# Second softmax group through GpSimd, logit sums on GpSimd, and router choices two per period, in a fused attention and mixture-of-experts kernel

## The chip, the core and the metric

The kernel runs on one core of a Trainium2 chip. The metric is the device time of one execution in microseconds (us), the median of several. The engines named below are TensorE (PE, with its weight loads shown apart as PEld), VectorE (DVE), ScalarE (ACT), GpSimd (POOL) and SyncE (SP, which here only issues DMAs).

## What is computed

Banded causal attention over 8 batches, 8 heads, 576 positions and head width 64 (window 64), and then a mixture of 8 experts over the 4608 tokens of 512 values. Tokens are given to experts by descending logit, each expert taking at most 576.

```python
scores = scale * np.matmul(q, k.transpose(0, 1, 3, 2))
mask = (rel >= 0) & (rel < window)
scores = np.where(mask, scores, -1000000000.0)
scores = scores - np.max(scores, axis=-1, keepdims=True)
attn = np.exp(scores)
attn = attn / (np.sum(attn, axis=-1, keepdims=True) + 1e-09)
x = np.matmul(attn, v)                  # then laid out as (4608, 512)
...
logits = x @ w_gate                     # (4608, 8)
order = np.argsort(-logits.flatten())   # greedy assignment, 576 tokens per expert
...
h = np.maximum(x[mask] @ w1[e], 0.0)    # for each expert e, on its tokens
out[mask] = h @ w2[e]
```

## The kernel before

**Stages.** Attention comes first (the change touches only this stage), then the routing of the first expert, then the products of the experts, with the routing of the later experts beside them. Nothing of the routing of expert 0 can begin before the last logits are there.

**Periods.** Queries are handled in 36 periods m = 0 to 35, two blocks of 64 queries each (one block per half of the 128 partitions), all 8 heads in two groups g = 0 and 1 of four heads. `S` is 576, so a batch b has nine blocks and its first one falls in period 9b/2 (rounded down). The loop is written out by hand as a software pipeline: the order in which it issues instructions is the order in which each engine runs them. In period m it issues:

- `qk(m, g)` (L118): 32 score matmuls on PE (L129); then on DVE, for each of 8 heads, one fused operation (L137) that adds the mask, scales by -1/8, writes `st` and accumulates the minimum into `mx` (so st is the negated scaled score and mx the negated row maximum). `st` has two buffers. A period's DVE work begins with these eight operations; the moment when the eighth has written its `mx` is called T(m) below.
- in some periods the gate products: `gate_mm` (PE, L86) with its copy `gate_cp` (ACT, L90) in the period where a batch begins, and in the next period `gate_tr` (PE, L96) and `gate_out`. The latter copies the products into `VO` (DVE, L102, L105) and then lets GpSimd build `VE`, the same rows of v shifted by one block, in eight copies per batch (`even`, L115 and L116). The periods with `gate_out` of a whole batch, called turning periods below, are 10, 14, 19, 23, 28 and 32 (batches 2 to 7).
- `pv(m - 2)` (PE, L169): 32 products of the exponentials with v. Besides the 64 values, the matmul yields the partial logits of 8 experts (columns 64 to 71) and the sum of the exponentials (column 72), into `Op`, which has one buffer.
- exponentials of group 0 (ACT, L142, one per head, with mx as the bias), `tr(m - 1)` (PE, L149: 8 transposes into `Tp`), and then on ACT two exponentials of group 1, the copy of the first `Tp` to `pt` (L151), two more exponentials, the copy of the second.
- `norm(m - 2)` (DVE): 1/sum (`r`, L198 and L199), the partial logits times r (`l`, L184), in every fourth period the sum over the eight heads into `L` (L188), and the values times r (`x`, L194). Between these four steps the loop puts one small operation each: those of `choices` (six operations on four columns of logits, which prepare the routing: m, G, oh, w, best, one) if any are waiting in `late`, else one of the generator `setup` (constants for the routing: tab, gt, sx, s and the like). At least two of the setup operations go into each period until they run out.
- DMA issues on SP: a store of x to DRAM, and in six periods the loads of a batch that comes later.

Of the kernel before, what the change touches and what calls it, by code (L numbers as in the profile page):

```python
# [9 lines left out]
FT = mybir.dt.float32  # L10
# [4 lines left out]
AF = mybir.ActivationFunctionType  # L15
OP = mybir.AluOpType
AX = mybir.AxisListType
# [5 lines left out]
E = 8  # L23
# [7 lines left out]
def attention(ctx, tc, c, q, k, v, vt, gate, xs, L, choices, setup, counters):  # L31

    nc = tc.nc
    wgbd, wg = gate
    ld = ctx.enter_context(tc.tile_pool(name="ld", bufs=2))
    wk = ctx.enter_context(tc.tile_pool(name="wk", bufs=3))
# [44 lines left out]
    def gate_mm(b, i0, i1):  # L81
        if not i0:
            VS[b] = wk.tile([128, S], FT, name="vs", bufs=2)
        pv = VS[b, i0] = ps.tile([128, 512], FT, name="Tp", bufs=2)
        for p in range(HP):
            nc.tensor.matmul(pv[32 * p:32 * p + 32, :64 * (i1 - i0)], wgbd[:, p, :],  # L86
                             VT[b][:, i0:i1, p], start=True, stop=True)

    def gate_cp(b, i0, i1):
        nc.scalar.activation(VS[b][:, 64 * i0:64 * i1], VS[b, i0][:, :64 * (i1 - i0)], AF.Copy)  # L90

    def gate_tr(b, i0, i1):
        pt = VS[b, i0] = ps.tile([128, 512], FT, name="Tp", bufs=2)
        for n, j in enumerate(range(i0 // 2, (i1 + 1) // 2)):
            w = 128 if j < 4 else 64
            nc.tensor.transpose(pt[:w, 128 * n:128 * n + 128], VS[b][:, 128 * j:128 * j + w], c["ident"])  # L96

    def gate_out(b, i0, i1):
        pt = VS[b, i0]
        j0, j1 = i0 // 2, i1 // 2  # L100
        n = j1 - j0
        nc.vector.tensor_copy(VO[b][:, j0:j1, :, 64:72],  # L102
                              pt[:, :128 * n].rearrange("p (j h g) -> p j h g", j=n, h=8)[:, :, :, :8])
        if i1 % 2:
            nc.vector.tensor_copy(VO[b][0:64, 4, :, 64:72],  # L105
                                  pt[:64, 128 * n:128 * n + 128].rearrange("p (h g) -> p h g", h=8)[:, :, :8])
        if not i0:
            VE[b] = ld.tile([128, 4, H, VW], FT, name="VE")
        for j in range(4):
            if i0 <= 2 * j + 2 < i1:  # L110
                even(b, j, nc.gpsimd if b or j > 1 else nc.vector)
# [6 lines left out]
    def qk(m, g):  # L118

        Sp = [t[g] for t in SP]  # L120
        bi = [divmod(2 * m + a, NB) for a in range(2)]
        for pp in range(2):
            p = 2 * g + pp
            for a, (b, i) in enumerate(bi):

                k0 = i - 1 if i else 0
                for r in range(2):
                    d = slice(64 * r, 64 * r + 64)
                    nc.tensor.matmul(Sp[r][64 * a:64 * a + 64, pp], Q[b][d, i, p],  # L129
                                     K[b][d, k0:k0 + 2, p], start=True, stop=True)  # L130
        kinds = [int(i > 0) for b, i in bi]
        mk = c["mask"][tuple(kinds)]
        st = wk.tile([128, 4, 128], FT, name="st", bufs=2)
        mx = wk.tile([128, 4], FT, name="mx")
        for h in range(4):

            nc.vector.tensor_tensor_reduce(st[:, h, :], Sp[h % 2][:, h // 2], mk, scale=-0.125, scalar=3.0e38,  # L137
                                           op0=OP.add, op1=OP.min, accum_out=mx[:, h:h + 1])
        pe = wk.tile([128, 4, 128], FT, name="pe", bufs=4)

        def exp(h):
            nc.scalar.activation(pe[:, h, :], st[:, h, :], AF.Exp, bias=mx[:, h:h + 1], scale=-1.0)  # L142

        return pe, [lambda h=h: exp(h) for h in range(4)]

    def tr(pe):
        Tp = ps.tile([128, 512], FT, name="Tp", bufs=2)
        for h in range(4):
            nc.tensor.transpose(Tp[:, 128 * h:128 * h + 128], pe[:, h, :], c["ident"])  # L149
        pt = wk.tile([128, 4, 128], FT, name="pt")  # L150
        return pt, lambda: nc.scalar.activation(pt.rearrange("p h q -> p (h q)"), Tp, AF.Copy)  # L151

    stores = []
    late = []
# [20 lines left out]
    def norm(m, Op):  # L175

        r = wk.tile([128, 2, 4], FT, name="r")
        x = wk.tile([128, H, D], FT, name="x", bufs=HOLD + 4)
        if m % 4 == 0:
            XL[0] = wk.tile([128, 4, H, E], FT, name="l", bufs=2)  # L180
        l = XL[0]

        def gates():
            nc.vector.tensor_tensor(l[:, m % 4].rearrange("p (g h) e -> p g h e", g=2), Op[:, :, :, 64:72],  # L184
                                    r[:, :, :, None].to_broadcast([128, 2, 4, E]), OP.mult)
            if m in ends:
                j0 = ends[m]
                nc.vector.tensor_reduce(L[:, j0:m + 1, :], l[:, j0 % 4:m % 4 + 1].rearrange("p i h e -> p i e h"),  # L188
                                        axis=AX.X, op=OP.add)
                if m != 34:  # L190
                    late.extend(choices(min(j0, 32), m + 1))

        def values():
            nc.vector.tensor_tensor(x.rearrange("p (g h) d -> p g h d", g=2), Op[:, :, :, 0:64],  # L194
                                    r[:, :, :, None].to_broadcast([128, 2, 4, 64]), OP.mult)
            stores.append((m, x))

        return [lambda: nc.vector.tensor_scalar(r, Op[:, :, :, 72], 1e-9, None, op0=OP.add),  # L198
                lambda: nc.vector.reciprocal(r, r), gates, values]  # L199
# [17 lines left out]
    def load_all(b):  # L217
        load_qk(b, *ALL)
        load_vt(b, *ALL)
        load_v(b, *ALL)  # L220

    M = B * NB // 2
# [15 lines left out]
    for m in range(M + 1):  # L238
        exps = [[], []]
        if m < M:  # L240
            P[m], exps = zip(*[qk(m, g) for g in range(2)])

        for x in products.get(m, []):
            gate_mm(*x)
        for x in turns.get(m, []):
            gate_tr(*x)
        for x in turns.get(m, []):
            gate_out(*x)
        Op = pv(m - 2, T.pop(m - 2)) if m > 1 else None
        for f in exps[0]:  # L250
            f()
        for x in products.get(m, []):
            gate_cp(*x)
        if m:
            T[m - 1], cps = zip(*[tr(pe) for pe in P.pop(m - 1)])
            for n, f in enumerate(exps[1]):
                f()
                if n % 2:
                    cps[n // 2]()
            if m == M:  # L260
                for f in cps:
                    f()
            if m == 1:
                for x in first:
                    gate_tr(*x)
                for x in first:
                    gate_out(*x)
        else:
            for f in exps[1]:
                f()  # L270
        more = [lambda: next(setup, None)] * (6 if m < 5 else 2)
        ops = norm(m - 2, Op) if Op is not None else []
        for f in ops:
            f()
            if late:
                late.pop(0)()
            elif more:
                more.pop()()
        for f in more:
            f()  # L280
        for s in (2 * m, 2 * m + 1):
            if stores and (len(stores) > HOLD or s > LOADED):
                store(*stores.pop(0))
        for b in loads.get(m, []):
            load_all(b)
# [80 lines left out]
class Routing:  # L366
# [90 lines left out]
    def choices(self, j0, j1, p):  # L457

        nc, V = self.nc, self.V
        r = slice(j0, j1)  # L460
        n = j1 - j0

        def wide(x):
            return x[:, r, None].to_broadcast([128, n, E])

        f = [lambda: nc.vector.tensor_reduce(self.m[:, r], V[:, r], axis=AX.X, op=OP.max),
             lambda: nc.vector.tensor_tensor(self.oh[:, r], V[:, r], wide(self.m), OP.is_equal),
             lambda: nc.vector.scalar_tensor_tensor(self.w[:, r], self.oh[:, r], 9.0,
                                                    self.cw9[:, None, :].to_broadcast([128, n, E]),
                                                    op0=OP.mult, op1=OP.add),  # L470
             lambda: nc.vector.tensor_reduce(self.best[:, r], self.w[:, r], axis=AX.X, op=OP.max),
             lambda: nc.vector.tensor_tensor(self.best[:, r], self.best[:, r], self.un[:, r], OP.mult),
             lambda: nc.vector.tensor_tensor(self.one[:, r], self.w[:, r], wide(self.best), OP.is_equal)]
        if not p:
            f.pop(4)
            f.insert(1, lambda: self.compare(self.G0, self.tab[:, 0], j0, j1))
        return f
# [603 lines left out]
```

## Time and profile before

| | us |
|---|---|
| median of 3 runs (661.39 to 663.77) | 663.59 |
| the profiled execution's own time | 665.81 |
| span of the profiled execution, first to last instruction | 664.2 |
| PE busy (matmul rows) | 623.3 |
| DVE busy | 441.6 |
| ACT busy | 356.9 |
| POOL busy | 187.2 |

The profile cannot chain the waits of this execution back beyond its last 11 us, so the attention stage has to be read from windows and from timelines: the order of instructions of one engine in a stretch, with the idle time before each. The stage runs from the first score matmuls at 4.7 us to the last division at about 161 us; the routing of expert 0 follows, in which PE is mostly idle, and from about 185 us to the end PE is busy without pause.

### The profile page before, as it was taken

To read this page: it belongs to the slowest core of one execution; us is meant where nothing else is said; L and a number is where in the kernel's file an instruction comes from. 1 tells how busy PE (TensorE), PEld (TensorE's weight loads), DVE (VectorE), ACT (ScalarE), POOL (GpSimd) and SP (SyncE) were. 2 spreads that over 40 slices of the span, in tenths; PEclk is the share of its full clock that TensorE was granted. 3 is DMA by queue.
4 is the path that set the end of the run, shared out by engine and by line. 5 is a ranking of instruction groups with operands and counts; after the bars stand their busy time and mean duration, and the time that the engine had idled before them with its cause. 6 is when DMAs were issued, how large, how long until landed. Compare 5 with 4: busy or idle time off the path is not lost. (4 is left out here: it accounts for less than half of the span.)

```text
span 664.2 us, 16832 instructions
## 1 busy us (share of the span) xinstructions
PE 623.3 (94%) x6383; PEld 535.6 (81%) x6383; DVE 441.6 (66%) x2102; ACT 356.9 (54%) x733; POOL 187.2 (28%) x218
## 2 busy tenths in 40 slices
PE   6989999996489999999999999999999999999995
PEld 4767787775379878987997898799889878989984
DVE  7798998887787767876885887588578741311300
ACT  5778898893056166336626543661744356635310
POOL 2223333330062042206305222530612155212111
PEclk9899999998589999999999999999999999999999
DMA  8999999721078189739748875965977598973401
GB/s 315 383 392 380 361 354 360 262 81 66 16 250 194 29 282 225 144 132 253 187 81 292 201 157 182 231 160 107 286 193 144 203 215 254 235 222 87 88 25 47
DMA packets 36016, 134.09 MB, mean 202 GB/s; under 512 B 4696, under 2 KB 4824, under 8 KB 32864
## 3 DMA queue, kind: packets, MB, share of 16 engines
q0 software_dynamic: 15280, 52.98, 35.5%
q1 hardware_dynamic: 20368, 79.52, 32.3%
q8 instruction: 50, 0.82, 0.5%
q10 hardware_dynamic: 288, 0.52, 0.3%
q14 instruction: 30, 0.25, 0.1%
HBM read 82.15 MB, written 18.87 MB: 152 GB/s over the span
## 5 line engine op out<-in xcount | busy, mean ns | idle before, releaser
L961 POOL DMA_INDIRECT out<-ot,idx x40 | 41.7, 1043 | 270.8 <-DVE ot L959 82.2
L911 ACT ACTIVATE hh<-h 128x256 fp32r<-128x256 f32 (+1 forms) x128 | 51.9, 408 | 101.1 <-PE h L939 99.8
L916 DVE SCALAR_TENSOR_TENSOR hl<-h,hh 128x256 fp32r<-128x256 f32 x128 | 53.2, 416 | 76.3 <-ACT hh L911 70.0
L981 PE MATMUL o<-wh,hh 128*128 128x512 f32 x256 | 102.5, 400 | 0.0
L981 PE MATMUL o<-wl,hh 128*128 128x512 f32 x256 | 101.8, 398 | 0.0
L981 PE MATMUL o<-wh,hl 128*128 128x512 f32 x256 | 101.4, 396 | 0.0
L142 ACT ACTIVATE pe<-st,mx 128x128 f32<-128x128 f32 x288 | 92.5, 393 | 14.8 <-DVE mx L137 14.8
L939 PE MATMUL h<-xh,wh 128*128 128x256 f32 (+1 forms) x512 | 92.0, 299 | 2.0 <-issue 1.0
L939 PE MATMUL h<-xh,wl 128*128 128x256 f32 (+1 forms) x512 | 93.0, 299 | 0.0
L939 PE MATMUL h<-xl,wh 128*128 128x256 f32 (+1 forms) x512 | 92.1, 298 | 0.4 <-DVE xl L874 0.4
L939 PEld LDWEIGHTS h<-xh,wh 128*128 128x128 f32 x512 | 75.8, 189 | 3.3 <-issue 1.1
L939 PEld LDWEIGHTS h<-xh,wl 128*128 128x128 f32 x512 | 76.1, 190 | 0.2
L939 PEld LDWEIGHTS h<-xl,wh 128*128 128x128 f32 x512 | 75.7, 190 | 0.7 <-DVE xl L874 0.6
L828 ACT ACTIVATE wh<-st 128x1024 fp32r<-128x1024 f32 x64 | 67.2, 1050 | 5.8 <-DMA st<-w 5.8
L137 DVE CUSTOM_DVE_ANT_0 st<-Sp,mask 128x128 f32<-128x128 f32 x288 | 63.7, 287 | 7.7 <-PE Sp L129 6.7
L839 POOL DMA_DIRECT2D wl<-st x61 | 56.6, 1231 | 35.3 <-ACT wl L837 24.1
L837 ACT ACTIVATE wl<-wh 128x1024 fp32r<-128x1024 f32 x61 | 64.4, 1056 | 0.8
L953 ACT ACTIVATE ot<-o 128x512 f32<-128x512 f32 x32 | 19.1, 598 | 84.1 <-PE o L981 80.9
L981 PEld LDWEIGHTS o<-wh,hl 128*128 128x128 f32 x256 | 48.1, 188 | 9.3 <-issue 0.4
L981 PEld LDWEIGHTS o<-wh,hh 128*128 128x128 f32 x256 | 48.3, 188 | 8.8
L981 PEld LDWEIGHTS o<-wl,hh 128*128 128x128 f32 x256 | 48.2, 188 | 8.6
L880 POOL DMA_INDIRECT xg<-xs,idx x40 | 41.4, 1036 | 45.5 <-DVE eq L724 35.1
(177 smaller groups left out, 1084.7 us busy)
## 6 DMA issues: line engine op xcount, KB each, us to landing
wl<-st POOLq DMA_DIRECT2D x61, 512.0 KB
st<-w SPq DMA_DIRECT2D x60, 512.0 KB
xs<-x SPq DMA_DIRECT2D x36, 256.0 KB
VO<-v SPq DMA_DIRECT2D x6, 1168.0 KB
Q<-q SPq DMA_DIRECT2D x6, 1152.0 KB
K<-k SPq DMA_DIRECT2D x6, 1152.0 KB
VT<-vt SPq DMA_DIRECT2D x6, 1152.0 KB
VO<-v SPq DMA_DIRECT2D x4, 584.0 KB
```

The lines of the kernel that those rows point to most:

```text
L137: nc.vector.tensor_tensor_reduce(st[:, h, :], Sp[h % 2][:, h // 2], mk, scale=-0.125, scalar=3.0e38, op0=OP.add, op1=OP.min, accum_out=mx[ ...
L142: nc.scalar.activation(pe[:, h, :], st[:, h, :], AF.Exp, bias=mx[:, h:h + 1], scale=-1.0)
L828: nc.scalar.activation(hi, st[i], AF.Copy)
L837: nc.scalar.activation(lo, hi.bitcast(FT), AF.Copy, scale=-1.0)
L839: nc.gpsimd.dma_start(lo.bitcast(FT), st[i], accum_op=OP.add)
L880: nc.gpsimd.indirect_dma_start(out=g[0:n, a], out_offset=None, in_=self.xs, in_offset=IndirectOffsetOnAxis(ap=idx[0:n, a:a + 1], axis=0))
L911: nc.scalar.activation(hh[:, f, c0:c1], h, AF.Relu)
L916: nc.vector.scalar_tensor_tensor(t, h[:, a - c0:b - c0], 0.0, hh[:, f, a:b].bitcast(FT), op0=OP.max, op1=OP.subtract)
L939: nc.tensor.matmul(h, wv[:, cc, 128 * (f % 2):128 * (f % 2) + 128], xt[:, cc, c0:c1], start=(k == 0), stop=(k == 11))
L953: nc.scalar.activation(ot, o, AF.Copy)
L961: nc.gpsimd.indirect_dma_start(out=self.out, out_offset=IndirectOffsetOnAxis(ap=idx[0:m, a:a + 1], axis=0), in_=ot[0:m], in_offset=None)
L981: nc.tensor.matmul(o, ht[:, f, 128 * a:128 * a + 128], wt[:, 512 * (f % 2):512 * (f % 2) + 512], start=(k == 0), stop=(k == 23))
```

## The change

Three edits, all within the loop of the attention stage.

**Exponentials of group 1.** In periods 0 to 34 `qk` issues, right behind the DVE operations of group 1, a GpSimd subtraction of mx from st over 128 x 512 elements, into `pe`. ACT then takes the exponential of all 512 columns in one instruction, in place. The loop issues it behind both copies of `Tp` rather than around the first.

**Sum over the heads.** For the 32 first periods three GpSimd additions (256 numbers of a row folded to 128, 64 and 32) take the place of the DVE reduction.

**Choices.** `norm`'s first two steps are followed by setup operations only; a waiting choice operation is put behind `l` and another behind `x`, two per period, and not in the period that produced them.

```diff
-        return pe, [lambda h=h: exp(h) for h in range(4)]
+        if not g or m == M - 1:
+            return pe, [lambda h=h: exp(h) for h in range(4)]
+        nc.gpsimd.tensor_tensor(pe, st, mx[:, :, None].to_broadcast([128, 4, 128]), OP.subtract)
+        return pe, [lambda: nc.scalar.activation(pe.rearrange("p h k -> p (h k)"), pe.rearrange("p h k -> p (h k)"),
+                                                 AF.Exp, scale=-1.0)]
...
-                nc.vector.tensor_reduce(L[:, j0:m + 1, :], l[:, j0 % 4:m % 4 + 1].rearrange("p i h e -> p i e h"),
-                                        axis=AX.X, op=OP.add)
+                if m < 32:
+                    a = wk.tile([128, 4, 4, E], FT, name="a", bufs=1)
+                    nc.gpsimd.tensor_tensor(a, l[:, :, 0:4], l[:, :, 4:8], OP.add)
+                    nc.gpsimd.tensor_tensor(a[:, :, 0:2], a[:, :, 0:2], a[:, :, 2:4], OP.add)
+                    nc.gpsimd.tensor_tensor(L[:, j0:m + 1, :], a[:, :, 0], a[:, :, 1], OP.add)
+                else:
+                    nc.vector.tensor_reduce(L[:, j0:m + 1, :], l[:, j0 % 4:m % 4 + 1].rearrange("p i h e -> p i e h"),
+                                            axis=AX.X, op=OP.add)
...
-            for n, f in enumerate(exps[1]):
+            for f in (*cps, *exps[1]):
                 f()
-                if n % 2:
-                    cps[n // 2]()
-            if m == M:
-                for f in cps:
-                    f()
...
-        for f in ops:
+        ready = len(late)
+        for n, f in enumerate(ops):
             f()
-            if late:
+            if n > 1 and ready:
                 late.pop(0)()
+                ready -= 1
             elif more:
                 more.pop()()
```

What stands in a row on the engines (line numbers of the changed kernel are its own: L147 is the new exponential, L146 the subtraction, L194 to L196 the additions, L155 the copy of `Tp`, L208, L209, L188 and L204 the steps of `norm`, L473 to L488 the choices, L451 to L456 setup). ACT, two periods before, the first of them one in which a batch begins:

```order
L142 ACTIVATE pe<-st,mx 128x128 x4
L90 ACTIVATE vs<-Tp 128x256
L90 ACTIVATE vs<-Tp 128x320
L142 ACTIVATE pe<-st,mx 128x128 x2
L151 ACTIVATE pt<-Tp 128x512
L142 ACTIVATE pe<-st,mx 128x128 x2
L151 ACTIVATE pt<-Tp 128x512
L142 ACTIVATE pe<-st,mx 128x128 x6
```

ACT now, the same place:

```order
L142 ACTIVATE pe<-st,mx 128x128 x4
L90 ACTIVATE vs<-Tp 128x256
L90 ACTIVATE vs<-Tp 128x320
L155 ACTIVATE pt<-Tp 128x512 x2
L147 ACTIVATE pe<-pe 128x512
L142 ACTIVATE pe<-st,mx 128x128 x4
```

The copies of `Tp` stand in front of group 1's exponential, and four instructions have become one. GpSimd now, periods 15 to 20 (batch 4's turning period 19 is among them; three further pairs of copies are left out):

```order
L146 TENSOR_TENSOR pe<-st,mx 128x512 x3
L194 TENSOR_TENSOR a<-l 128x128
L195 TENSOR_TENSOR a<-a 128x4x16
L196 TENSOR_TENSOR L<-a 128x32
L146 TENSOR_TENSOR pe<-st,mx 128x512 x2
L115 COPY VE<-VO 64x584
L116 COPY VE<-VO 64x584
...
L146 TENSOR_TENSOR pe<-st,mx 128x512 x2
```

Before, this engine had only the copies of VE in this stage. The subtraction of period 20 now stands behind the eight copies of period 19. DVE before, behind the eight operations of a turning period (10):

```order
L102 COPY VO<-Tp 128x16x8 x2
L105 COPY VO<-Tp 64x8x8
L198 TENSOR_SCALAR r<-Op 128x8
L467 TENSOR_TENSOR oh<-L,m 128x32
L199 RECIPROCAL r<-r 128x8
L468 SCALAR_TENSOR_TENSOR w<-oh,cw_219 128x32
L184 TENSOR_TENSOR l<-Op,r 128x64
L471 TENSOR_REDUCE best<-w 128x4
L194 TENSOR_TENSOR x<-Op,r 128x512
L473 TENSOR_TENSOR one<-w,best 128x32
L449 TENSOR_TENSOR s_674<-sx_939,sx_1030 72x5
L444 TENSOR_SCALAR sx_1139<-jp 72x4
```

DVE now, the same place:

```order
L102 COPY VO<-Tp 128x16x8 x2
L105 COPY VO<-Tp 64x8x8
L208 TENSOR_SCALAR r<-Op 128x8
L456 TENSOR_TENSOR s_662<-sx_922,sx_1013 72x5
L209 RECIPROCAL r<-r 128x8
L451 TENSOR_SCALAR sx_1115<-jp 72x4
L188 TENSOR_TENSOR l<-Op,r 128x64
L473 TENSOR_REDUCE m<-L 128x4
L204 TENSOR_TENSOR x<-Op,r 128x512
L488 TENSOR_TENSOR G_76<-m,tab 128x60
```

The two setup operations have moved from the end to the places ahead of `l`, and choices come two at a time. In the built program the first DVE operation of a period, which writes group 0's `st`, now waits for GpSimd's subtraction of the period before: the two buffers of `st` are handed on in the order in which they are released, and the subtraction is issued before the exponentials of group 0. Before, both groups' operations waited for ACT.

## Rows read from the trace of the kernel before

**Rows 1.** The profile's page: busy time of the engines, and the span in 40 slices (busy share in tenths; PEclk is TensorE's granted clock).

```profile
PE 623.3 (94%) x6383; PEld 535.6 (81%) x6383; DVE 441.6 (66%) x2102; ACT 356.9 (54%) x733; POOL 187.2 (28%) x218
...
PE   6989999996489999999999999999999999999995
DVE  7798998887787767876885887588578741311300
ACT  5778898893056166336626543661744356635310
PEclk9899999998589999999999999999999999999999
```

**Rows 2.** Busy time of each engine in windows (us, then PE, PEld, DVE, ACT, POOL busy, granted clock, DMA share, GB/s): one plain period, nine periods in a row, the two halves of the loop, the routing of expert 0.

```profile
78.40:81.70 3.30, 3.30 (x77) 2.82 (x74) 2.83 (x23) 3.30 (x11) 0.00 (x0) 1.00 0.91 332
...
75.12:108.51 33.39, 32.88 (x674) 26.38 (x672) 30.26 (x217) 31.46 (x95) 9.65 (x15) 1.00 0.95 346
...
30.97:96.76 65.79, 61.18 (x1236) 48.85 (x1230) 58.91 (x393) 56.58 (x168) 21.69 (x32) 1.00 0.99 372
96.76:151.30 54.54, 52.06 (x1077) 42.09 (x1075) 47.06 (x320) 49.20 (x147) 16.08 (x24) 1.00 0.63 235
...
158.60:185.00 26.40, 11.89 (x329) 10.15 (x326) 19.18 (x97) 1.53 (x2) 1.07 (x1) 0.54 0.17 57
```

**Rows 3.** Timeline of PE's weight loads, periods 20 to 24 (start, duration, line, names; in brackets idle time before and its releaser; rows of `pv` are left out). L149 is `tr`, L86 `gate_mm`, L96 `gate_tr`.

```profile
91.16 0.86 PEld L149 LDWEIGHTS Tp<-ident,pe 128*128 128x128 f32 x8
...
94.39 0.86 PEld L149 LDWEIGHTS Tp<-ident,pe 128*128 128x128 f32 x8
95.42 0.86 PEld L129 LDWEIGHTS Sp<-K,Q 64*64 64x64 f32 x32 [0.17 <-issue]
97.63 0.86 PEld L149 LDWEIGHTS Tp<-ident,pe 128*128 128x128 f32 x8
...
99.69 0.16 PEld L86 LDWEIGHTS Tp<-VT,wgs 128*32 128x32 f32 x8 [0.17 <-ACT pe L142]
...
100.89 0.13 PEld L169 LDWEIGHTS Op<-VE,pt 128*64 128x64 f32 x1 [0.52 <-issue]
...
102.07 0.86 PEld L149 LDWEIGHTS Tp<-ident,pe 128*128 128x128 f32 x8
...
106.19 0.86 PEld L149 LDWEIGHTS Tp<-ident,pe 128*128 128x128 f32 x8
```

**Rows 4.** Timeline of ACT: the start of period 5, a whole plain period (17, with what comes ahead of it), and the start of period 35. Instructions of one kind in a row are merged (x6).

```profile
30.97 1.28 ACT L142 ACTIVATE pe<-st,mx 128x128 f32<-128x128 f32 x4
...
78.43 1.85 ACT L142 ACTIVATE pe<-st,mx 128x128 f32<-128x128 f32 x6
80.18 0.58 ACT L151 ACTIVATE pt<-Tp 128x512 f32<-128x512 f32 x1
80.66 0.69 ACT L142 ACTIVATE pe<-st,mx 128x128 f32<-128x128 f32 x2
81.24 0.59 ACT L151 ACTIVATE pt<-Tp 128x512 f32<-128x512 f32 x1
81.72 1.86 ACT L142 ACTIVATE pe<-st,mx 128x128 f32<-128x128 f32 x6
...
151.30 1.85 ACT L142 ACTIVATE pe<-st,mx 128x128 f32<-128x128 f32 x6
```

**Rows 5.** Waits from 41 to 156 us, sums over the stretch: who waited for whom, us in total, times, longest.

```profile
PEld Op L169 <- issue: 4.6, 13, 1.0
PEld Sp L129 <- issue: 4.1, 16, 1.6
...
PEld Tp L86 <- ACT pt L151: 2.0, 6, 0.4
...
PEld Op L169 <- POOL VE L116: 1.4, 2, 0.7
...
PEld Tp L96 <- ACT pt L151: 1.3, 6, 0.2
```

**Rows 6.** Timeline of GpSimd and DVE around copies of VE: the first copy behind its DVE copy in period 5, then GpSimd's first and last copy of turning period 19.

```profile
32.11 0.28 DVE L102 COPY VO<-Tp 128x128 f32<-128x128 f32 x1
...
32.45 0.67 POOL L115 COPY VE<-VO 64x584 f32<-64x584 f32 x1 [5.91 <-DVE VO L102]
...
90.99 0.67 POOL L115 COPY VE<-VO 64x584 f32<-64x584 f32 x1 [13.41 <-issue]
...
96.05 0.67 POOL L116 COPY VE<-VO 64x584 f32<-64x584 f32 x1
```

**Rows 7.** Timeline of DVE, periods 19 to 21: the end of period 19's eight operations, period 20's `r` and `x`, the first of period 21's eight and the end of the last.

```profile
90.58 0.08 DVE L137 DVE_READ_ACCUMULATOR2_ANT mx<- 128x1 f32 x1
...
94.70 0.16 DVE L198 TENSOR_SCALAR r<-Op 128x8 f32<-128x8 f32 x1
...
95.34 0.67 DVE L194 TENSOR_TENSOR x<-Op,r 128x512 f32<-128x512 f32 x1
96.25 0.29 DVE L137 CUSTOM_DVE_ANT_0 st<-Sp,mask 128x128 f32<-128x128 f32 x1 [0.23 <-PE Sp L129]
...
97.94 0.09 DVE L137 DVE_READ_ACCUMULATOR2_ANT mx<- 128x1 f32 x1
```

**Rows 8.** Timeline of GpSimd and DVE: a GpSimd copy, two small DVE operations that ran beside such a copy, two of the same kinds with GpSimd idle, and, in the view of line 137, the eight operations' durations over the stage (ns, least, median, most).

```profile
55.34 0.67 POOL L115 COPY VE<-VO 64x584 f32<-64x584 f32 x1 [14.14 <-DVE VO L102]
...
55.54 0.52 DVE L467 TENSOR_TENSOR oh<-L,m 128x32 bf16<-128x32 f32 x1
...
33.28 0.59 DVE L444 TENSOR_SCALAR sx<-jp 72x5 f32<-72x5 int32 x1
...
87.23 0.18 DVE L467 TENSOR_TENSOR oh<-L,m 128x32 bf16<-128x32 f32 x1
...
88.71 0.17 DVE L444 TENSOR_SCALAR sx<-jp 72x4 f32<-72x4 int32 x1
...
L137 DVE CUSTOM_DVE_ANT_0 st<-Sp,mask x288: 279/286/293, 6.2 to 152.3; 128x128 f32<-128x128 f32 x144
```

**Rows 9.** Groups of instructions by line and shape (count | busy us, mean ns of one | idle before).

```profile
L188 DVE TENSOR_REDUCE L<-l 128x32 f32<-128x256 f32 x8 | 5.0, 628 | 0.3
```

## The prediction

> **What bounds the kernel now.** I read the page first: over the whole span PE is busy 94%, but its slices show that the first tenth and the gap after the attention stage are weaker, and ACT and DVE are at seven to nine tenths in the stage that the change touches [rows 1]. So which of three nearly full engines sets the pace there has to be read from single periods. A plain period (17) is 3.30 us long; PE and ACT are both busy for all of it, DVE for 2.83 [rows 2]. ACT's stream has no gap there either: 6 exponentials, copy, 2 exponentials, copy, from 78.43 to 81.72, 3.29 us [rows 4]. Had ACT alone set the pace, PE would show waits. It shows almost none: the transposes of periods 21, 22 and 23 start at 91.16, 94.39 and 97.63, 3.23 us apart, with only the 0.17 us gaps that stand at every change of operand [rows 3]. From 75.12 to 108.51 PE is busy 32.88 of 33.39 us [rows 2]. PE therefore has a floor of its own of 3.23 us per period; a period with gate products takes 102.07 - 97.63 = 4.44 and the turning period behind it 106.19 - 102.07 = 4.12 [rows 3], which adds 1.21 + 0.89 = 2.10 per batch. ACT is as late as PE, not later.
>
> **What can be gained.** From the start of period 5 to that of period 35 before takes 151.30 - 30.97 = 120.3 us [rows 4]. The floor for these 30 periods is 30 x 3.23 = 96.9, plus 6 x 2.10 = 12.6 for batches 2 to 7, plus about 1.5 for the rest of batch 1's gates: 111.0. So 9.3 us lie above PE's floor. Of these, two stalls of 1.6 and 1.0 have no releaser at all (the longest of the two "issue" waits [rows 5]); no edit here touches them. Another 1.4 is PE waiting for copies of VE on GpSimd [rows 5], which the change makes no shorter. That leaves 5.3; I take 5 as gained. PE's waits for ACT inside the gate stages, 2.0 + 1.3 us [rows 5], may shrink a little, since the Tp copies now precede the long exponential: I take 1, between 0 and 3.3.
>
> **Group 1's exponentials.** Two exponentials merged on ACT last 0.69, of six 1.85 [rows 4], so each further one costs (1.85 - 0.69)/4 = 0.29. Four are 1.16; one instruction of 512 columns costs about what the copy of Tp does, 0.58 at most. ACT gets about 0.6 us per period, 35 times 0.6 = 21 us of ACT time. Nearly all of it is worth nothing, since PE keeps its 3.23; what it buys is in the 5 above.
>
> **The subtraction.** The trace has no two-operand GpSimd operation. Nearest is the copy of 584 numbers in 0.67 [rows 6]: 512 at that pace are 0.59, one operand. With two operands to be read I take it twice, S = 1.2; bounds 0.6 (as a copy) and 1.4 (twice, and stretched). The Trainium skill, page "GPSIMD Engine Reference", section 3.1 (elementwise, side by side), gives 4497 ns for an addition of 2048 fp32 columns; a quarter of that would be an estimated 1.1, and the sum below would come out 1 us lower. No row here shows it.
>
> In a plain period S is hidden: it starts some 0.07 after the last maximum (a copy started at 32.45 behind a DVE copy that ended at 32.39 [rows 6]), the exponential follows, and PE asks for group 1 only 2.9 us and more after the eighth DVE operation (94.70 to 97.63, and four transposes come first [rows 3, 7]). DVE's next period waits for the subtraction too, but 0.07 + 1.2 is what its division takes anyway (94.70 to about 95.95 [rows 7]). If that cover fails (S above about 1.4), the loop of eight operations and subtraction, 1.77 + S + 0.1, passes 3.23 and every period pays.
>
> **The turning periods, which decide it.** Here GpSimd's queue holds the subtraction, then eight copies of VE, then the next period's subtraction. Take batch 4 (period 19). T(19) = 90.58 + 0.08 = 90.66 [rows 7]. The copies last from 90.99 to 96.72, 5.73 us [rows 6]. Now they begin after the subtraction, and the next subtraction ends at 90.66 + 0.07 + S + 5.73 + 0.05 + S = 96.51 + 2S, or 98.9. Two things wait for that.
> First, ACT's exponential (0.1 + 0.59, done 99.6), for which PE asks at 97.63 + 0.43 = 98.06 [rows 3]: 1.5 late, and ACT's next exponentials and copies stand behind it.
> Second, DVE: period 21's first operation may not write st before that subtraction is done. It started at 96.25 [rows 7], and now at 99.0, so T(21) is 100.75 instead of 98.03, and the division that follows it ends at about 102.0; the next pv needs Op back from it. PE would have begun that pv at 100.89 behind gate products [rows 3], or at about 99.7 in a batch without them there.
> Following both to the next transposes: about 103.7 instead of 102.07 where gate products fall in between (batches 2, 4, 6), 1.6 us; 103.2 instead of 100.87 where they don't (3, 5, 7), 2.3 us. PE has nothing above its floor with which to make this up. Mean 2.0, six batches: **12 us**. With S = 0.6 the same steps give 0.3 and 1.2, so 4.5; with S = 1.4, 2.0 and 2.8, so 14.4. Batch 1's copies fall where the loop is still slow, and I count nothing.
>
> **Sum over heads and choices.** Eight reductions of 0.63 [rows 9] leave DVE, seven or eight times; the sum of their gain is inside the 5, since DVE was late only in those periods. GpSimd's three small additions (each at most the 0.67 of a copy) run after the period's subtraction and before the next, and hide. Choices two per period shift DVE work out of the turning periods; also inside the 5.
>
> **Contention.** Beside a GpSimd copy, DVE's oh took 0.52 and sx 0.59, against 0.18 and 0.17 with GpSimd idle, and that oh ended at 56.06 with the copy at 56.01; the eight operations of L137 stay within 279 to 293 ns throughout [rows 8]. The Trainium skill, page "GPSIMD Engine Reference", section 1 (specifications), says that GpSimd shares its SBUF interfaces with VectorE and contends with DVE operations in a two-port mode or with two SBUF inputs. By that rule, the trace agrees for oh, and rival (d) would follow if every subtraction held the interface to its end. From the rows alone: the second setup operation of a period, or oh, which stand ahead of x, would now wait for the subtraction's end, up to 0.85 us; a period of 1.77 + 1.25 + 0.85 = 3.87 is 0.64 above PE's floor. Outside the stretches that turning periods delay anyway some three plain periods pay: 2 us, between 0 (it holds for copies only) and 5 (eight plain periods).
>
> **Sum.** -5 - 1 + 12 + 2 = +8. The tail (routing onward, 26.4 us at a mean granted clock of 0.54, so mostly at the lower level of 1.2 GHz, and then the experts [rows 2]) follows the attention stage rigidly: nothing of it is started earlier. The profiled execution took 665.8, 2.2 above the median; 665.8 + 8 = 673.8, or **671.6** against the median of 663.6.
>
> **Rivals.**
> (a) Forecast: the queue behind VE's copies decides, +4 to +12. For it: order and 5.73 us. Against it: S is not in the trace. 0.50.
> (b) The subtraction is quick and the stalls only eat the gain: at S of about 0.72 the mean stall is 1.0, six of them cancel the 6 gained, and the time stays at 664. For it: a copy's pace. 0.22.
> (c) Faster: the same place from the other side. Below S = 0.72 the gain wins; at 0.6 with all of 5.3 and 3.3 coming and no contention, 4.5 - 8.6 = -4, a time of 659. For it: ACT's relief is real. Against it: two operands at a one-operand pace. 0.14.
> (d) Contention dominates: DVE waits for the subtraction in all periods with setup, and S is 1.4: 14.4 + 5 - 4 = +15, 679. 0.14.
> That the edits don't do what they say is excluded by the built order.
>
> **Chances and range.** A difference below 0.5% (3.3 us) cannot be told from none here. Faster 0.14 (c), same 0.23 (b and the edge of a), slower 0.63 (the rest of a, and d). The range leaves out the last part of (c) and of (d): 661 to 679.
>
> **What would show it.** After: in each of periods 11, 15, 20, 24, 29, 33 GpSimd's subtraction begins right behind a copy of VE; ACT's 512-column exponential and DVE's first operation of the next period wait for POOL 1 to 3 us; PE's transposes around them are 5 us apart and more, and 3.2 elsewhere. L146 near 1.2 us. Wrong, if L146 takes 0.7 or less, if PE shows no waits behind turning periods, or if plain periods fall below 3.2, since then the floor isn't PE's.

## The result, and the profile after

| | median us | from | to | runs |
|---|---|---|---|---|
| before | 663.43 | 661.39 | 663.77 | 4 |
| changed | 671.34 | 670.36 | 672.41 | 4 |

The ratio is 1.0126, with a 95% interval of 1.0104 to 1.0148: slower by 7 to 10 us. The forecast was 671.6. The profiled execution of the changed kernel took 671.14, 0.2 below its median, while that of before (665.81) lay 2.4 above the median of this table; the two traces therefore differ by 5.3 only, 2.6 less than the medians.

First the page: busy times over the whole span, to be read against [rows 1].

```profile
PE 622.4 (93%) x6383; PEld 536.1 (80%) x6383; DVE 440.5 (66%) x2094; ACT 338.0 (50%) x628; POOL 231.1 (35%) x277
```

ACT has 18.9 us less to do, GpSimd 43.9 more, and PE the same. Next the groups of instructions by line (count | busy us, mean ns of one | idle before, and what ended it): the eight operations per period on DVE, the subtraction, the merged exponential, the first of the three additions.

```profile
L137 DVE CUSTOM_DVE_ANT_0 st<-Sp,mask 128x128 f32<-128x128 f32 x288 | 63.6, 286 | 19.2 <-POOL pe L146 14.0 <-PE Sp L129 4.5
...
L146 POOL TENSOR_TENSOR pe<-st,mx 128x512 f32<-128x512 f32 x35 | 36.5, 1042 | 60.9 <-DVE mx L137 33.8 <-PE Sp L129 9.6 <-ACT vs L90 5.4
...
L147 ACT ACTIVATE pe<-pe 128x512 f32<-128x512 f32 x35 | 21.9, 627 | 20.4 <-POOL pe L146 20.4
L194 POOL TENSOR_TENSOR a<-l 128x128 f32<-128x128 f32 x8 | 3.6, 454 | 1.2 <-DVE l L188 1.1
```

One subtraction takes 1.04 us; DVE and ACT stand idle behind it for 14.0 and 20.4 us, where before, in this stage, only PE waited for GpSimd, 2.1 us in all. The view of waits from 30 to 162 us (us in total, times, longest) says how often, and what it does to PE. (A stall of PE shows in its weight loads and again in its matmuls, so the two rows of PE are the same stalls and don't add up.)

```profile
ACT pe L147 <- POOL pe L146: 19.1, 14, 2.8
...
DVE st L137 <- POOL pe L146: 14.0, 6, 3.0
...
PEld Tp L153 <- ACT pe L147: 6.4, 6, 1.6
...
PE Tp L153 <- ACT pe L147: 5.0, 5, 1.4
```

DVE waits six times, 2.3 us in the mean: once behind each turning period of batches 2 to 7, each time ahead of the first of its eight operations. For batch 4 the place is shown by the timeline of several engines (start, duration, line; in brackets the idle time before).

```profile
90.29 1.04 POOL L146 TENSOR_TENSOR pe<-st,mx 128x512 f32<-128x512 f32 x1 [3.30 <-DVE mx L137]
91.40 0.72 POOL L115 COPY VE<-VO 64x584 f32<-64x584 f32 x1
...
96.46 0.67 POOL L116 COPY VE<-VO 64x584 f32<-64x584 f32 x1
97.21 1.04 POOL L146 TENSOR_TENSOR pe<-st,mx 128x512 f32<-128x512 f32 x1
98.28 0.63 ACT L147 ACTIVATE pe<-pe 128x512 f32<-128x512 f32 x1 [2.82 <-POOL pe L146]
98.28 0.29 DVE L137 CUSTOM_DVE_ANT_0 st<-Sp,mask 128x128 f32<-128x128 f32 x1 [2.55 <-POOL pe L146]
```

The subtraction of period 20 begins right behind the eighth copy, and ACT's exponential and DVE's first operation start in the same moment, 0.03 after it. PE's transposes around it, which answer to [rows 3]:

```profile
93.67 0.86 PEld L153 LDWEIGHTS Tp<-ident,pe 128*128 128x128 f32 x8
...
97.52 0.42 PEld L153 LDWEIGHTS Tp<-ident,pe 128*128 128x128 f32 x4
98.96 0.42 PEld L153 LDWEIGHTS Tp<-ident,pe 128*128 128x128 f32 x4 [1.03 <-ACT pe L147]
...
103.42 0.86 PEld L153 LDWEIGHTS Tp<-ident,pe 128*128 128x128 f32 x8 [0.51 <-ACT vs L90]
...
107.35 0.75 PEld L153 LDWEIGHTS Tp<-ident,pe 128*128 128x128 f32 x7
```

Group 0's four transposes run on time, group 1's wait 1.03 for the exponential, and the next eight come at 103.42: 5.90 behind the last, against 4.44 for a period with gate products before. The turning period behind it is 107.35 - 103.42 = 3.93, shorter than the 4.12 of before. The six stalls are not alike: the same interval is 5.8 to 6.5 us in batches 2, 4 and 6, where gate products fall into it, and 4.3 (batch 3) to 5.7 in batches 3, 5 and 7, where it would be a plain period. Plain periods that nothing disturbs stay at 3.23 to 3.24. Windows with the same ends as in [rows 2] (start of period 5 to 21, to 35, and the routing; us, then busy time of PE, PEld, DVE, ACT, POOL, granted clock, DMA share, GB/s):

```profile
31.01:98.82 67.81, 61.65 (x1260) 50.43 (x1256) 58.78 (x391) 47.58 (x119) 42.30 (x60) 1.00 1.00 373
98.82:156.12 57.30, 51.33 (x1046) 41.46 (x1048) 44.90 (x312) 41.42 (x105) 34.56 (x50) 1.00 0.56 207
163.30:190.00 26.70, 12.27 (x331) 10.37 (x328) 19.54 (x100) 1.53 (x2) 1.07 (x1) 0.55 0.18 59
```

The first half takes 2.0 us more, the second 2.8 more, and the routing behind them is nearly as it was (26.7 us at a granted clock of 0.55, against 26.4 at 0.54). Of the 5.3 us between the two traces 4.8 lie in the attention stage.

### The profile page after: what moved, and what is told of

Same layout as the page of the kernel before. It is cut to its first block, busy times and chain, and to the rows that moved or that the text cites. A ratio compares the mean times of both kernels' runs of the same rounds, so it can differ in the third digit from the quotient of the medians.

```text
span 669.5 us, 16842 instructions
## 1 busy us (share of the span) xinstructions
PE 622.4 (93%) x6383; PEld 536.1 (80%) x6383; DVE 440.5 (66%) x2094; ACT 338.0 (50%) x628; POOL 231.1 (35%) x277
## 5 line engine op out<-in xcount | busy, mean ns | idle before, releaser
L137 DVE CUSTOM_DVE_ANT_0 st<-Sp,mask 128x128 f32<-128x128 f32 x288 | 63.6, 286 | 19.2 <-POOL pe L146 14.0
L146 POOL TENSOR_TENSOR pe<-st,mx 128x512 f32<-128x512 f32 x35 | 36.5, 1042 | 60.9 <-DVE mx L137 33.8
```

The costliest lines, as they stand in the source:

```text
L146: nc.gpsimd.tensor_tensor(pe, st, mx[:, :, None].to_broadcast([128, 4, 128]), OP.subtract)
```

## The experiments

Each kernel ran in its own rounds beside the kernel before; times of different rounds are compared by their ratio to it, and "us" below is (ratio - 1) x 663.6. The difference of two ratios carries about 2 us either way.

| kernel | median us | ratio (95%) | us |
|---|---|---|---|
| changed | 671.34 | 1.0126 (1.0104 to 1.0148) | +8.4 |
| e1_copies_spread | 663.24 | 0.9983 (0.9961 to 1.0005) | -1.1 |
| e2_no_sub_behind_copies | 662.85 | 0.9990 (0.9971 to 1.0009) | -0.7 |
| e3_sums_choices_only | 661.23 | 0.9957 (0.9934 to 0.9979) | -2.9 |
| e4_exp_only | 676.88 | 1.0205 (1.0170 to 1.0239) | +13.6 |
| e5_st_four | 667.16 | 1.0063 (1.0048 to 1.0078) | +4.2 |
| e6_exp_only_spread | 669.79 | 1.0095 (1.0071 to 1.0119) | +6.3 |
| e7_sums_choices_order | 664.77 | 1.0016 (0.9995 to 1.0036) | +1.1 |
| e8c_spread_e7 | 665.73 | 1.0036 (1.0018 to 1.0054) | +2.4 |
| e8_idle_sub | 667.44 | 1.0065 (1.0043 to 1.0087) | +4.3 |
| e9_merge_gates_only | 661.24 | 0.9967 (0.9956 to 0.9979) | -2.2 |
| e10_dve_waits_only | 667.62 | 1.0062 (1.0042 to 1.0082) | +4.1 |
| e11_e2_st_four | 664.03 | 0.9991 (0.9973 to 1.0009) | -0.6 |

Theory A: the subtraction queued behind VE's copies makes the loss. Theory B: GpSimd's work beside DVE makes it (contention). Theory C: one exponential that waits for a subtraction comes later than four small ones did.

**The queue taken apart in two ways.** In e1 the copies of VE are issued one pair per period, behind which no subtraction waits long.

```diff
-                even(b, j, nc.gpsimd if b or j > 1 else nc.vector)
+                if b:
+                    shifts.append((b, j))
+                else:
+                    even(b, j, nc.gpsimd if j > 1 else nc.vector)
...
+        if shifts:
+            even(*shifts.pop(0), nc.gpsimd)
```

> The changed kernel with the eight copies of VE of batches 1 to 7 issued one pair per period over four periods, instead of all in the turning period. Theory A (the subtraction queued behind the eight copies makes the loss): no subtraction stands behind more than one pair (1.4 us), the six stalls of 1 to 2.5 us go, and some 10 us come back: 661, or 2 to 3 below the kernel before. Theory B (GpSimd's subtraction and sums slow DVE through their shared interface, in all periods): the copies still run beside as many DVE operations, and the time stays at 668 to 671. Theory C (the subtraction's latency is paid in every period): 668 to 671, plain periods above 3.3 us.

It is -1.1, so 9.5 us came back by the ratios (8.1 by the medians). Its waits from 30 to 162 us and PE's transposes at batch 4:

```profile
ACT pe L151 <- POOL pe L150: 1.5, 4, 0.6
...
DVE st L141 <- POOL pe L150: 0.4, 1, 0.4
```

```profile
93.03 0.86 PEld L157 LDWEIGHTS Tp<-ident,pe 128*128 128x128 f32 x8
96.33 0.85 PEld L157 LDWEIGHTS Tp<-ident,pe 128*128 128x128 f32 x8
100.67 0.86 PEld L157 LDWEIGHTS Tp<-ident,pe 128*128 128x128 f32 x8
104.60 0.85 PEld L157 LDWEIGHTS Tp<-ident,pe 128*128 128x128 f32 x8
```

ACT's 19.1 us have become 1.5, DVE's 14.0 have become 0.4, and the transposes come 3.30, 4.34 and 3.93 apart, with no stall. In e2 the copies stay in a block, and the six periods behind them do without the subtraction.

```diff
-        if not g or m == M - 1:
+        if not g or m in (11, 15, 20, 24, 29, 33, M - 1):
```

> The changed kernel, but in the six periods behind a turning period (11, 15, 20, 24, 29, 33) group 1's four exponentials stay on ACT with mx as their bias, with no subtraction. Copies stay in one burst. Theory A: nothing waits for GpSimd behind the copies, about 9 to 10 us come back: 661 to 663. Theory B or C: 29 of 35 subtractions are still there, so at most 2 us come back: 669 to 670.

It is -0.7. Taking away the copies or the subtraction from that one place gives the same: theory A holds, at 9 to 9.5 us, and B and C, which asked for 668 and more in both kernels, can't be the main cause.

**Which of the two waiters.** The prediction named ACT's exponential and DVE's first operation. e5 gives `st` four buffers, so that DVE no longer needs the last subtraction; e10 is e2 with a subtraction back in the six periods into a tile that nobody reads, so that DVE waits for it and ACT doesn't; e11 is e2 with e5's buffers, the control of e5.

```diff
-        st = wk.tile([128, 4, 128], FT, name="st", bufs=2)
-        mx = wk.tile([128, 4], FT, name="mx")
+        st = wk.tile([128, 4, 128], FT, name="st", bufs=4)
+        mx = wk.tile([128, 4], FT, name="mx", bufs=8)
```

```diff
         if not g or m in (11, 15, 20, 24, 29, 33, M - 1):
+            if g and m < M - 1:
+                idle = wk.tile([128, 4, 128], FT, name="idle", bufs=1)
+                nc.gpsimd.tensor_tensor(idle, st, mx[:, :, None].to_broadcast([128, 4, 128]), OP.subtract)
             return pe, [lambda h=h: exp(h) for h in range(4)]
```

(To make room, `HOLD`, which sets how many finished tiles of x are kept, is 14 in e5 and e11 and 15 in e10, against 16 elsewhere.)

> The changed kernel with four buffers of st instead of two (and eight of mx): DVE's first operation of a period no longer waits for the subtraction just before it, while ACT's exponential still does. The queue behind VE's copies stays. If ACT's wait alone holds PE up (the first of the prediction's two waiters), 669 to 672, as the changed kernel's 671.3. If DVE's wait is the one that costs (the second), 663 to 666. If each gives about half, 666 to 669.

> The complement: in the six periods behind the block of copies ACT keeps its four small exponentials and waits for no subtraction, but GpSimd still runs one there into a tile that nobody reads, so DVE's first operation of the period after still waits for it. Without that idle subtraction the kernel took 662.9. If DVE's wait is the one that costs, 668 to 671; if ACT's is, 663 to 665; half each, 665 to 668.

> Control for the four buffers: the kernel that took 662.9 (no subtraction in the six periods behind the block of copies), with four buffers of st and eight of mx. Here nothing late is waited for, so 662 to 664 by either theory; if it is faster than that, the buffers help DVE elsewhere, and this, not 662.9, is what the run with four buffers and the queue is to be compared with.

Waits from 30 to 162 us, first of e5, then of e10, and DVE's timeline at batch 4 in e10:

```profile
ACT pe L147 <- POOL pe L146: 17.0, 7, 2.8
...
DVE m L473 <- POOL L L196: 3.0, 2, 1.5
DVE st L137 <- POOL L L196: 2.8, 2, 1.5
```

```profile
DVE st L137 <- POOL idle L147: 7.6, 5, 1.8
```

```profile
95.20 0.28 DVE L137 CUSTOM_DVE_ANT_0 st<-Sp,mask 128x128 f32<-128x128 f32 x1
...
95.83 0.28 DVE L137 CUSTOM_DVE_ANT_0 st<-Sp,mask 128x128 f32<-128x128 f32 x1
...
97.84 0.29 DVE L137 CUSTOM_DVE_ANT_0 st<-Sp,mask 128x128 f32<-128x128 f32 x1 [1.72 <-POOL idle L147]
```

With ACT's wait alone the kernel is 4.2 + 0.6 = 4.8 above its control (3.1 by the medians), with DVE's alone 4.1 + 0.7 = 4.8 above e2 (4.8 by the medians). So both waiters cost, 3 to 5 us when either is left alone, and both together the 9. The two times lie where they were expected if each gives about half, but that split isn't shown, because neither kernel isolates its waiter cleanly. In e10 it isn't the first operation of the period that waits, as was expected, but the fifth: four run from 95.20 on, and the fifth starts at 97.84. Group 1's `st` is read there by ACT's exponentials too, which come behind those of group 0, so that buffer is handed on last. DVE waits 7.6 us in five places, where in the changed kernel it waits 14.0 in six. And in e5 DVE still stood 5.8 us for GpSimd, in four places, which the trace puts down to the sums (L196), twice ahead of `st` and twice ahead of the choice `m`. The buffers alone changed nothing (e11).

**What the rest of the change is worth.** e3 keeps the sums and the choices and takes the subtraction, the merged exponential and the new order of ACT's copies away (shown against the changed kernel).

```diff
-        if not g or m == M - 1:
-            return pe, [lambda h=h: exp(h) for h in range(4)]
-        nc.gpsimd.tensor_tensor(pe, st, mx[:, :, None].to_broadcast([128, 4, 128]), OP.subtract)
-        return pe, [lambda: nc.scalar.activation(pe.rearrange("p h k -> p (h k)"), pe.rearrange("p h k -> p (h k)"),
-                                                 AF.Exp, scale=-1.0)]
+        return pe, [lambda h=h: exp(h) for h in range(4)]
...
-            for f in (*cps, *exps[1]):
+            for n, f in enumerate(exps[1]):
                 f()
+                if n % 2:
+                    cps[n // 2]()
...
```

> The kernel before with only the sums over the heads on GpSimd and the choices two per period; exponentials and their order as before. Theory A: no subtraction, no stall; DVE is relieved of 0.63 us in eight periods, worth 0 to 2: 661 to 663.5. Theory B: the sums and moved choices cost part of the loss: 665 to 668.

e4 is the reverse: it has all that this diff takes away, and the sums and choices of before.

```diff
-                if m < 32:
-                    a = wk.tile([128, 4, 4, E], FT, name="a", bufs=1)
...
+                nc.vector.tensor_reduce(L[:, j0:m + 1, :], l[:, j0 % 4:m % 4 + 1].rearrange("p i h e -> p i e h"),
+                                        axis=AX.X, op=OP.add)
...
-            if n > 1 and ready:
+            if late:
                 late.pop(0)()
-                ready -= 1
```

> The kernel before with only the subtraction, the one exponential of 512 columns and the Tp copies ahead of it; sums and choices as before. Theory A: the stalls are all there and DVE's late periods remain: 671 to 674. Theory B: without the sums and the moved choices part of the loss goes: 667 to 669.

e3 is the fastest, -2.9; e4 +13.6. So the gain of the whole change is in the sums and choices, and the merged exponential adds nothing to it that can be seen: e1, which has it without the queue, is 1.8 slower than e3, within the 2 us. The next four kernels ask why. e7 adds to e3 the order alone, both copies of `Tp` ahead of the four exponentials:

```diff
-            for n, f in enumerate(exps[1]):
+            for f in (*cps, *exps[1]):
                 f()
-                if n % 2:
-                    cps[n // 2]()
...
```

> Sums on GpSimd and choices two per period, as in the run that took 661.2, and now also both copies of Tp ahead of group 1's four exponentials; no subtraction and no merged exponential. If the turning periods became shorter (4.12 to 3.93 us) because the copies come earlier, the same 3.93 here and 659 to 660.5. If they became shorter because ACT has three instructions fewer, 4.1 and 661 to 663.

It is 4.0 slower than e3, and the turning periods were 4.22, not shorter. Its waits of DVE from 41 to 156 us:

```profile
DVE st L137 <- ACT pe L142: 5.2, 21, 0.3
DVE st L137 <- ACT pt L151: 4.0, 12, 0.5
```

In the kernel before, DVE waited 0.9 us for ACT there in all. With the copies first, ACT reads `st` later, and DVE's next period waits for that in 33 places. In the changed kernel this price isn't paid, because there the subtraction releases `st`.

e8c spreads the copies of VE in e7, and e8 adds one subtraction per period that reads the mask and `mx`, writes a tile that nobody reads, and is waited for only where a buffer of `mx` comes round again; for that `mx` has eight buffers in e8 and `HOLD` is 15, which its control e8c doesn't share.

```diff
+        if g and m < M - 1:
+            idle = wk.tile([128, 4, 128], FT, name="idle", bufs=1)
+            nc.gpsimd.tensor_tensor(idle, mk[:, None, :].to_broadcast([128, 4, 128]),
+                                    mx[:, :, None].to_broadcast([128, 4, 128]), OP.subtract)
         return pe, [lambda h=h: exp(h) for h in range(4)]
```

> The kernel with sums, choices and early copies of Tp, and VE's copies spread, one pair per period; the control for the next run. Nothing on GpSimd is in a hurry here, so the spread should change little: within 1 us of the kernel that it is made from; up to 1.4 us faster if PE's waits for VE go.

> The control with one GpSimd subtraction of 128x512 per period more, into a tile that nobody reads; the four exponentials stay on ACT as they are. It reads the mask tile and mx, and nobody waits for it except mx's buffers, of which there are now eight. If GpSimd's work beside DVE costs by itself (the prediction's contention, 2 us, 0 to 5), it is 2 to 5 us slower than the control, with small DVE operations at 0.4 to 0.6 us beside it. If contention is hidden, within 1 us.

The spread alone is 1.3 slower than e7, which is within the 2 us. The idle subtraction costs 1.9 us (4.3 - 2.4), about as much as two such ratios can be apart by chance, so a cost of nothing isn't excluded. What it does can be seen on one setup operation, in the groups from 41 to 150 us, first of e8c, then of e8 (line numbers of each kernel):

```profile
L458 DVE TENSOR_TENSOR s<-sx,sx 72x5 bf16<-72x5 f32 x6 | 1.7, 276 | 0.0
```

```profile
L462 DVE TENSOR_TENSOR s<-sx,sx 72x5 bf16<-72x5 f32 x7 | 5.3, 755 | 0.0
```

e6 is e4 with the copies spread (the diffs of e4 and e1 together), so subtraction and merged exponential without the queue, but with choices where they were before.

> The subtraction and the merged exponential alone (no sums on GpSimd, choices as before), with VE's copies spread over the periods, one pair in each. With the copies in a block this part alone took 676.9. If the queue behind the block of copies makes all of its loss, 663 to 667 here. If the relief of ACT is worth the 5 to 6 us that the prediction took, 658 to 660. If GpSimd's work beside DVE costs something by itself, or the merged exponential comes later than four small ones, 668 and more.

It is +6.3: the queue's share of e4's loss is 13.6 - 6.3 = 7.3, and 6.3 remain that e1 doesn't have. Without the subtraction, sums and choices gain 2.9 (e3); with it they gain 6.3 + 1.1 = 7.4. Two operations of the choices, in the groups from 41 to 150 us, of e6 and of e1:

```profile
L472 DVE TENSOR_TENSOR oh<-L,m 128x32 bf16<-128x32 f32 x6 | 4.3, 720 | 0.0
...
L473 DVE SCALAR_TENSOR_TENSOR w<-oh,cw 128x32 bf16<-128x32 bf16 x6 | 4.0, 665 | 0.0
```

```profile
L480 DVE TENSOR_TENSOR oh<-L,m 128x32 bf16<-128x32 f32 x7 | 1.9, 276 | 0.0
L481 DVE SCALAR_TENSOR_TENSOR w<-oh,cw 128x32 bf16<-128x32 bf16 x7 | 1.3, 185 | 0.0
```

Where choices stand between r and l, `oh` and `w` fall beside GpSimd's work and take 0.72 and 0.67; behind l and x they take 0.28 and 0.19. That is 0.9 us in each period that has both, ahead of x, and PE's next `pv` waits for x. The net is less, since the setup operation `s`, which stands ahead of `l` in e1, rises from 0.35 in e6 to 0.54. That the moved choices and not the moved sums make the 4.5 us between 7.4 and 2.9 was not tried apart; these durations speak for it.

**The merged exponential only where it shortens a period.** e9 uses it in the twelve periods of the gate products and the turning alone, and else before's order.

```diff
-        if not g or m == M - 1:
+        if not g or m not in (9, 10, 13, 14, 18, 19, 22, 23, 27, 28, 31, 32):
...
-            for f in (*cps, *exps[1]):
+            e = exps[1]
+            for f in (*cps, *e) if len(e) < 2 else (*e[:2], cps[0], *e[2:], cps[1]):
```

> Sums on GpSimd, choices two per period, and the subtraction with the merged exponential only in the twelve periods where a batch's gate products and its turning period lie (9 and 10, 13 and 14, and so on), copies of Tp first there; elsewhere the four exponentials around the copies. No subtraction stands behind a block of copies. If the merged exponential is worth the 0.29 us per batch by which gate and turning periods became shorter, 661.2 less 1.7, so 659 to 660; if it gains nothing anywhere, 661 to 663; over 664, it costs even here.

It is -2.2, like e3 within the intervals. Its turning periods do take 3.93, but nothing of the 1.7 us expected from that can be seen in the time, which differs from e3's by less than the 2 us. e3 and e9 both beat the kernel before by 2 to 3 us, and are the versions to keep.

## Why the prediction came out right

The time and the deciding mechanism held: the forecast's case (a). But two terms were wrong in opposite directions, the gain by 3 us and the queue by 2.5 to 3, and their errors nearly cancel. That the forecast of 671.6 came within 0.3 us is luck; that it fell in the middle of case (a) is not.

- **PE's floor** of 3.23 held in the undisturbed plain periods of every kernel here.
- **S** was taken as 1.2; L146 takes 1.04. The prediction's own steps give 4.5 at 0.6 and 12 at 1.2, so about 10 at 1.04. Measured are 9.5 (e1) and 9.0 (e2). (An estimate from the Trainium skill, page "GPSIMD Engine Reference", section 3.1, was 1.1 by its 4497 ns for four times the columns; the trace's 1.04 is close to it.) The mechanism, the places and both waiters were as told; the 12 was too large by what S was. "5 us apart and more" holds for five of the six places (batch 3: 4.3). Rivals (b) and (c), which needed S of 0.72 or less, fell with it.
- **The gain** was taken as 5 + 1. It is 2.9, all of it present in e3, with ACT as before. The term that was mis-sized is "That leaves 5.3; I take 5 as gained": it gave all the idle time above PE's floor that had a releaser other than GpSimd to the edits together, without saying which wait each of them ends. The sums and choices alone gain the 2.9, and ACT's relief adds nothing that can be seen (the waits are shown behind this list). The 18.9 us of ACT time that were saved bought no shorter period, except in the gate stages (4.12 to 3.93, 4.44 to 4.34), where the predicted 1 is the right size by the transposes, though e9's time doesn't show it.
- **Contention** of 2 against 1.9 in e8, give or take 2: the size fits, but for an incomplete reason. The prediction put the move of the choices inside the gain; by the durations of `oh` and `w` it is probably what keeps contention at 2. With sums and choices in their old places the kernel pays 4.5 more (7.4 - 2.9). Rival (d) was nearer than it looked.
- **Sums**: 0.45, 0.32 and 0.25 us, each below the bound of 0.67, and hidden in the main (e3 has them and is faster).
- **The tail** followed to within 0.7 us: the last transposes start at 160.02 instead of 155.42, 4.6 later, and the profiled execution ends 5.3 later.

**Where the gain lies.** PE's waits ahead of `pv` from 41 to 156 us, some of them, first before, then in e3, then in e1 (us in total, times, longest):

```profile
PEld Op L169 <- ACT pt L151: 2.5, 4, 0.8
...
PEld Op L169 <- ACT pe L142: 1.9, 6, 0.7
...
PE Op L169 <- DVE G L481: 1.4, 3, 0.5
...
PE Op L169 <- DVE x L194: 1.1, 2, 0.6
```

```profile
PE Op L169 <- DVE w L476: 0.2, 1, 0.2
```

```profile
PE Op L177 <- DVE w L481: 3.7, 4, 1.4
```

Before, the matmuls of `pv` wait 2.5 us for DVE, and in e3 0.2 of that is left. The waits for ACT there, of matmuls and weight loads, are no smaller: 5.5 before, 6.3 in e3, 5.4 in e1. That fits a gain made by DVE's relief. In e1, beside the subtractions, the waits for DVE come to 5.0 (w 3.7, one 1.1, x 0.2), which fits contention. Neither is proof: these are single traces, and in one stall the matmuls and the weight loads can be put down to different engines, so the sums overlap and are not time gained.

The sum in measured terms: -2.9, +9.5 and +1.9 make +8.5, and -0.1 is left for the merged exponential to reach the measured 8.4. That rest is what the others leave over (e1 - e3 - 1.9), so the sum closes by construction, and with some 2 us on each term it says only that the merged exponential is worth nothing that these runs can tell from zero. What stays open: the stalls of PE without a releaser, up to 2.3 us each, which fall in other places in every trace; how the queue's 9 us divide between ACT's and DVE's waits; whether the gain of 2.9 comes from the sums or from the choices; and why the shorter turning periods of e9 don't reach its time.

## What to carry to other kernels

Before work goes to an engine that looks idle, list what else stands in its in-order queue: 5.7 us of copies were harmless for as long as nobody waited for what came behind them, and spreading them cost one line. Time freed on an engine that is only as late as the bounding one is not a gain until a wait of the bounding engine can be named that it ends. And where GpSimd is made to work in each period, try DVE's small operations in the places where it is idle; here the durations speak for it, and no run tried it alone.

## What the runs showed of the hardware

A small DVE operation that starts beside a GpSimd instruction can last until that instruction ends. The timeline of e6 shows it twice in a row:

```profile
122.14 0.67 POOL L119 COPY VE<-VO 64x584 f32<-64x584 f32 x1
122.16 0.69 DVE L472 TENSOR_TENSOR oh<-L,m 128x32 bf16<-128x32 f32 x1
...
122.86 0.67 POOL L120 COPY VE<-VO 64x584 f32<-64x584 f32 x1
122.89 0.69 DVE L473 SCALAR_TENSOR_TENSOR w<-oh,cw 128x32 bf16<-128x32 bf16 x1
```

The copy ends at 122.81 and `oh` at 122.85; the next copy at 123.53 and `w` at 123.58. In e8 the setup operation s does the same beside the idle subtraction:

```profile
62.86 0.97 DVE L462 TENSOR_TENSOR s<-sx,sx 72x5 bf16<-72x5 f32 x1
```

The subtraction runs from 62.78 for 1.04, to 63.82, and s ends at 63.83. It is not a matter of two operands alone: in e4 a setup operation with one operand (int32 to fp32) began 0.14 behind a subtraction and lasted to 68.36, where the subtraction ended at 68.33.

```profile
67.29 1.04 POOL L146 TENSOR_TENSOR pe<-st,mx 128x512 f32<-128x512 f32 x1 [1.98 <-DVE r L202]
67.43 0.93 DVE L443 TENSOR_SCALAR sx<-jp 72x5 f32<-72x5 int32 x1
```

The Trainium skill, page "GPSIMD Engine Reference", section 1 (specifications), has GpSimd share its SBUF interfaces with VectorE, with contention in a two-port mode or with two SBUF inputs; the traces agree for `oh`, `w` and s, and whether the two-port mode is what holds the setup operation, no run here shows. The eight operations of L137, which read scores and mask, keep their 0.29 in all of this (median 0.285 in the changed kernel, most 0.293), and x keeps its 0.68.

A GpSimd subtraction of 128x512 with two operands took 1.04 us where a copy of 64x584 took 0.67. One exponential of 512 columns took 0.63 as the trace has it, against 1.26 for four of 128 columns. From start to start it is 0.54 (98.28 to 98.82), against 1.17 for the four (98.82 to the next start at 99.99).
